# Weight conversion in a fused attention and two-layer MoE kernel: sign extraction of every third pair and more of the low parts moved from VectorE to GpSimd

## The chip, the core and the metric

The kernel runs on one core of a Trainium2 chip. TensorE multiplies matrices into PSUM; VectorE, ScalarE and GpSimd work element by element; SyncE (SP) issues the DMA transfers. The metric is the device time of one execution in microseconds, the median of several runs.

## The reference

Three steps follow each other: attention in which each query keeps its 32 best keys, a gated layer, and a layer with a squared ReLU. The attention's inputs are float32, the weights float64.

```python
def _attn_ref(q, k, v):                       # 4 batches, 8 heads, 576 x 64
    scores = scale * np.matmul(q, k.transpose(0, 1, 3, 2))
    kth = np.partition(scores, -32, axis=-1)[..., -32:-31]
    scores = np.where(scores >= kth, scores, -1000000000.0)
    scores = scores - np.max(scores, axis=-1, keepdims=True)
    attn = np.exp(scores)
    attn = attn / (np.sum(attn, axis=-1, keepdims=True) + 1e-09)
    return np.matmul(attn, v)
def _moe_ref(x, w_gate, w_val, w_out):        # x 2304 x 512, d_ff 1536
    gate = 1.0 / (1.0 + np.exp(-(x @ w_gate)))
    return (gate * (x @ w_val)) @ w_out
def _moe2_ref(x, w_in, w_out):                # d_ff 2048
    r = np.maximum(x @ w_in, 0.0)
    return (r * r) @ w_out
```

## The kernel before

The 2304 tokens are 18 row blocks of 128. Six blocks are a chunk each, the other twelve are taken in pairs (`CHUNKS`). For each chunk the attention runs over four pairs of heads, then the two layers. One head on one row block is a unit: on VectorE it is four MAX8 and three MATCH_REPLACE8 over 576 scores (L388, L395), which give the 32nd best score; GpSimd makes the small factors from it (L403, L404, L427), ScalarE the mask and the exponential (L407, L423), TensorE the scores and products.

The weights come in as float64, 128x512 to a block, two blocks to a pair; the five matrices wg, wv, wo, wi and w2 have 6, 6, 6, 8 and 8 pairs, 34 in all. `conv` makes float32 from a pair with integer arithmetic on the two 32-bit words. ScalarE copies the high word scaled by 2^-112 (L606) and the low word scaled (L625). VectorE shifts the pair left by three (L620, one operation over 128x1024) and ORs the sign of the high word into each block (L621, two operations of 128x512). GpSimd adds the low word (L626, two of 128x512). The sign is bit 31 of the high word, which is every second word of the raw tile.

Chunk 0 uses these float32 weights. For all other chunks `split` makes two float16 halves: ScalarE the high part (L661), and VectorE in one operation of 128x1024 (L664) or GpSimd in two (L666, L667) the low part. Every third low part goes to GpSimd (`LOP = 3`).

The order on each engine is not written out. A tile scheduler sets it from priorities: the code puts the weight steps, the units of the attention and the steps of chunk 0 on a time axis (`at`), and the scheduler orders each engine's queue by its own estimate. Each engine then runs its queue strictly in that order. The list of splits alternates between wg and wv, then goes to wo, wi and w2. Raw blocks and converted pairs share the slots of one pool (`WSLOTS`), so a later load waits until the add of an earlier pair has read its raw block.

For each chunk a maximum sets the scale of its input (x_1cm for chunk 1, L704) and another one that of the second layer's input (x2cm, L827); both are read on VectorE.

Of the kernel before, what the change touches and what calls it, by code (L numbers as in the profile page):

```python
# [15 lines left out]
ALU = mybir.AluOpType  # L16
# [31 lines left out]
SM2 = ()  # L48
XUP = 1000
DIAG = 2  # L50
SGN = 0
M4RAW = 0
KEYS1 = 1
SWI = 5
# [4 lines left out]
WSLOTS = 35  # L59
PREF = 4  # L60
YMOD = 0
LOP = 3
LOA = 0
TCI = 6
SB = 5
# [8 lines left out]
def tile_topk_attention__then__two_moe_layers(  # L74
# [14 lines left out]
    nc = tc.nc  # L89
# [469 lines left out]
    nblk = [0]  # L559
# [5 lines left out]
    def fetch_to(i):  # L565
        while fetched[0] < len(blocks):
            b = fetched[0]
            spare = b >= len(blocks) - M4RAW
            if b > i and not (b <= i + PREF and (spare or live[0] + 3 <= WSLOTS)):
                break  # L570
            n, kt, fb = blocks[b]
            src = weights[n][kt * P : (kt + 1) * P, fb * 512 : (fb + 1) * 512]
            pool, kw = (mpool, {"tag": "m4", "bufs": M4}) if spare else (wpool, {"tag": "w"})
            if src.dtype == F32:
                t = pool.tile([P, 512], F32, name=f"{n}_r{kt}_{fb}", **kw)
                nc.sync.dma_start(t, src)
            else:
                t = pool.tile([P, 512, 2], U32, name=f"{n}_r{kt}_{fb}", **kw)
                nc.sync.dma_start(t.rearrange("p f t -> p (f t)"), src.bitcast(U32))
            if not spare:  # L580
                live[0] += 1
            raws[(n, kt, fb)] = t
            fetched[0] += 1

    def conv(name, pi):

        pr = pairs_of[name][pi]
        fetch_to(blocks.index((name, *pr[-1])))
        if (name, pi) in CM4:
            c = mpool.tile([P, 2, 512], F32, tag="m4", bufs=M4, name=f"{name}_c{pi}")  # L590
        else:
            c = wpool.tile([P, 2, 512], F32, tag="w", name=f"{name}_c{pi}")
            live[0] += 1
        rs = [raws.pop((name, kt, fb)) for kt, fb in pr]
        ci = c.bitcast(U32)
        wide = weights[name].dtype != F32
        for e, r in enumerate(rs):
            nblk[0] += 1
            if not wide:
                nc.gpsimd.tensor_copy(c[:, e], r)  # L600
            elif YMOD and nblk[0] % YMOD == 0:
                nc.gpsimd.tensor_scalar(
                    c[:, e], r.bitcast(F32)[:, :, 1], REBIAS, 1.0, op0=ALU.mult, op1=ALU.mult
                )
            else:
                nc.scalar.activation(c[:, e], r.bitcast(F32)[:, :, 1], AF.Copy, scale=REBIAS)  # L606
        if wide:
            for e, r in enumerate(rs):
                hi = r[:, :, 1]
                if SGN and nblk[0] % SGN == 0:  # L610

                    nc.gpsimd.tensor_scalar(
                        hi.bitcast(F32), hi.bitcast(F32), 0.0, 1.0, op0=ALU.mult, op1=ALU.mult
                    )
                    nc.vector.scalar_tensor_tensor(
                        ci[:, e], ci[:, e], 3, hi, op0=ALU.logical_shift_left, op1=ALU.bitwise_or
                    )
                else:
                    if e == 0:
                        nc.vector.tensor_scalar(ci, ci, 3, None, op0=ALU.logical_shift_left)  # L620
                    nc.vector.scalar_tensor_tensor(  # L621
                        ci[:, e], hi, 0x80000000, ci[:, e], op0=ALU.bitwise_and, op1=ALU.bitwise_or
                    )
                low = r[:, :, 0].bitcast(I32)
                nc.scalar.activation(low, r[:, :, 0], AF.Copy, scale=float(2.0**-29))  # L625
                nc.gpsimd.tensor_tensor(  # L626
                    c.bitcast(I32)[:, e], c.bitcast(I32)[:, e], low, op=ALU.add
                )
        live[0] -= sum(blocks.index((name, *b)) < len(blocks) - M4RAW for b in pr)
        for e, (kt, fb) in enumerate(pr):  # L630
            flat[(name, kt, fb)] = (c, e)
# [25 lines left out]
    def split(name, pi):  # L657
# [4 lines left out]
        nsp[0] += 1  # L662
        if not (LOP and nsp[0] % LOP == 0 and nsp[0] > LOA):
            nc.vector.scalar_tensor_tensor(t[:, 1], c, s, t[:, 0], op0=ALU.mult, op1=ALU.subtract)  # L664
# [9 lines left out]
    def weight_step(n=1):  # L674
        for _ in range(min(n, len(steps) - nstep[0])):
            name, pi = steps[nstep[0]]
            conv(name, pi)
            nstep[0] += 1
            if name in ("wg", "wv", "wo") and pi == len(pairs_of[name]) - 1:
                scale(name)  # L680
# [605 lines left out]
```

## Time and profile before

| what | us |
|---|---|
| median of three runs | 1292.55 (1292.32 to 1298.61) |
| the profiled execution | 1289.27 |
| its span, first to last instruction | 1287.5 |
| TensorE matmul busy | 1175.5 (91%) |
| VectorE busy | 977.1 (76%) |
| GpSimd busy | 889.7 (69%) |
| ScalarE busy | 812.0 (63%) |

The shares are averages over stages. The stages are: up to 33 us the first keys and scores; 33 to 200 us the conversion of the weights beside the attention of chunks 0 and 1; 200 to some 310 us the splits, the end of chunk 0 and the first layer of chunk 1; from there on chunk after chunk, with the attention of a later chunk beside the layers of an earlier one, until the attention ends near 1100 us. In the rows PE is TensorE, DVE VectorE, ACT ScalarE, POOL GpSimd.

### The profile page before, as it was taken

Reading aid. Unit: us, or ns where it says so; the run is one execution under the profiler, and the core shown is the slowest. Engines: PE = TensorE matmul, PEld = TensorE weight load, DVE = VectorE, ACT = ScalarE, POOL = GpSimd, SP = SyncE. Lnnn points to the kernel's source line nnn. Section 1 sums busy time; section 2 is a strip of 40 time slices with the busy share of each in tenths; the row PEclk is TensorE's granted clock in tenths of the full one; section 3 lists DMA queues with packets and bytes.
Section 4 is the critical chain, followed back from the end, with each engine's and each line's share of the span. In section 5 each row is a group of like instructions: output and inputs, shape, how many; then the busy total and the mean of one; then the engine's idle time right before and its main releaser. Section 6 shows DMA issues by size and latency. Waiting matters only on the chain.

```text
span 1287.5 us, 31379 instructions
## 1 busy us (share of the span) xinstructions
PE 1175.5 (91%) x11709; PEld 945.3 (73%) x11709; DVE 977.1 (76%) x2002; ACT 812.0 (63%) x1714; POOL 889.7 (69%) x1454
## 2 busy tenths in 40 slices
PE   6756888877999989899998999999999999999998
PEld 5544876666887968778786778876876887787775
DVE  5999998999669987879998778999999969210010
ACT  4877777777666776667766776766676657322122
POOL 1798878876656677687876977798779759514223
PEclk9567899996999999999998999999999999999999
DMA  6978862222444346655666565556544523200000
GB/s 179 355 256 278 282 201 62 64 74 73 135 124 114 87 119 150 138 133 122 131 139 160 120 132 126 125 134 146 108 93 88 128 55 60 54 1 1 17 1 17
DMA packets 243192, 153.97 MB, mean 120 GB/s; under 512 B 193120, under 2 KB 209504, under 8 KB 243040
## 3 DMA queue, kind: packets, MB, share of 16 engines
q1 hardware_dynamic: 243040, 151.97, 45.9%
q8 instruction: 92, 1.51, 0.5%
q14 instruction: 60, 0.49, 0.1%
HBM read 105.51 MB, written 18.09 MB: 96 GB/s over the span
## 4 chain that ended last, share of the span: by engine, by line
PE 50%; DVE 20%; POOL 8%; DMA 8%; issue 6%; ACT 5%; SPq 2%; POOLq 0%; ACTq 0%; DVEq 0%
PE ph L855 11%; PE acc L876 10%; DVE mx L388 8%; DVE W L395 7%; PE pv L752 6%; PE pg L752 6%; PE acc L792 6%; PE sp L373 4%; PE xp L505 3%; DMA PT<-S 2%; PE xp L532 2%; DMA ve<-in_v_dram 1%; DMA vd<-vom 1%; POOL S L453 1%; POOL rh L868 1%
## 5 line engine op out<-in xcount | busy, mean ns | idle before, releaser
L388 DVE MAX8 mx<-W 128x8 f32<-128x576 f32 x432 | 327.3, 758 | 10.0
L395 DVE MATCH_REPLACE8 W<-mx,W 128x576 f32<-128x576 f32 x288 | 213.7, 742 | 0.0
L855 PE MATMUL ph<-x,wi_w 128*128 128x256 f16 (+1 forms) x2112 | 206.6, 251 | 5.1 <-ACT x L831 4.5
L876 PE MATMUL acc<-w_w,rh 128*128 128x512 f16 x816 | 198.5, 380 | 5.5 <-POOL rh L868 5.5
L855 PEld LDWEIGHTS <-wi_w 128*128 128x128 f16 x2112 | 170.7, 99 | 35.7 <-issue 6.2
L752 PE MATMUL pg<-xs,wg_w 128*128 128x256 f16 (+1 forms) x1584 | 158.8, 250 | 2.0 <-ACT xs L519 1.1
L752 PE MATMUL pv<-xs,wv_w 128*128 128x256 f16 (+1 forms) x1584 | 155.3, 249 | 2.6 <-DVE x2cm L827 2.5
L373 PE MATMUL sp<-kst,qt 128*128 128x288 f32 x608 | 136.2, 335 | 12.9 <-DMA kst<-ks 4.5
L407 ACT ACTIVATE W<-S,bs 128x576 f32<-128x576 f32 x144 | 111.8, 776 | 54.7 <-POOL bs L403 54.1
L752 PEld LDWEIGHTS <-wg_w 128*128 128x128 f16 x1584 | 126.9, 98 | 19.9 <-issue 1.9
L752 PEld LDWEIGHTS <-wv_w 128*128 128x128 f16 x1584 | 125.7, 98 | 18.8 <-issue 5.1
L453 POOL TENSOR_TENSOR S<-W,S 128x512 f16<-128x512 f32 x192 | 136.7, 734 | 2.1
L792 PEld LDWEIGHTS <-wo_w 128*128 128x128 f16 x1584 | 125.6, 98 | 13.1 <-issue 0.9
L876 PEld LDWEIGHTS <-rh 128*128 128x128 f16 x816 | 75.6, 98 | 78.6 <-POOL rh L868 6.8
L764 DVE TENSOR_TENSOR th<-pv,th 128x512 f32<-128x512 f32 (+1 forms) x66 | 37.0, 561 | 118.8 <-PE pv L752 117.7
L376 ACT COPY S<-sp 128x576 f32<-128x576 f32 x144 | 91.7, 637 | 55.8 <-PE sp L373 38.0
L388 DVE MAX8 mx<-S 128x8 f32<-128x576 f32 x144 | 107.0, 743 | 24.6 <-ACT S L376 24.6
L867 POOL TENSOR_TENSOR r<-r 128x512 f32<-128x512 f32 (+1 forms) x88 | 74.3, 845 | 63.4 <-ACT rh L866 57.5
L792 PE MATMUL acc<-gh,wo_w 128*128 128x128 f16 (+1 forms) x1248 | 114.3, 244 | 1.1 <-POOL gh L768 0.8
L373 PEld LDWEIGHTS sp<-kst,qt 128*128 128x128 f32 x608 | 92.4, 196 | 25.5 <-DMA kst<-ks 6.2
L395 DVE MATCH_REPLACE8 W<-mx,S 128x576 f32<-128x576 f32 x144 | 106.8, 742 | 0.0
L450 ACT ACTIVATE S<-W,rz 128x576 f16<-128x576 f32 x96 | 74.4, 775 | 48.7 <-DVE rz L446 44.9
(300 smaller groups left out, 2250.4 us busy)
## 6 DMA issues: line engine op xcount, KB each, us to landing
kst<-ks SPq DMA_DIRECT2D x112, 288.0 KB, 3.2
v<-vd SPq DMA_DIRECT2D x32, 320.0 KB, 3.2
qn<-in_q_dram SPq DMA_DIRECT2D x128, 64.0 KB, 2.6
wi_r<-in_moe_w_in_dram SPq DMA_DIRECT2D x16, 512.0 KB, 6.9
w_r<-in_moe_w_out_dram SPq DMA_DIRECT2D x16, 512.0 KB, 4.2
v<-in_v_dram SPq DMA_DIRECT2D x56, 128.0 KB, 2.4
wg_r<-in_moe_w_gate_dram SPq DMA_DIRECT2D x12, 512.0 KB, 8.0
wv_r<-in_moe_w_val_dram SPq DMA_DIRECT2D x12, 512.0 KB, 6.5
```

The source lines that it names most:

```text
L373: nc.tensor.matmul(sp[:, e, 0:HALF], l, r, start=(x == 0), stop=(x == len(ops) - 1))
L376: nc.scalar.copy(ss.rearrange("p (e s) -> p e s", e=2), sp[:, :, 0:HALF])
L388: m8 = nc.vector.max(mx[:, r], cur)
L395: nc.vector.match_replace(wk, mx[:, r], cur, NEG)
L407: nc.scalar.activation(wk, ss, AF.Prelu, bias=bs[:, 0:1], scale=1.0, alpha=BIG)
L450: nc.scalar.activation(pp[:, 0:S], wk, AF.Copy, scale=rz)
L453: nc.gpsimd.tensor_tensor(pp[:, o : o + e - f], wk[:, f:e], pp[:, f:e], op=ALU.subtract)
L752: nc.tensor.matmul(pp[:, e * N : (e + 1) * N], wblk(wd, a, c, f0, P), xs[:, b_, c, :], start=(e == 0 and n == 0), stop=(n == 3 * KM - 1), ...
L792: nc.tensor.matmul(acc[:, d // 2, (d % 2) * N : (d % 2 + 1) * N], wblk("wo", a, f, d * P, P), gh[:, b_, e * N : (e + 1) * N], start=(f == ...
L855: nc.tensor.matmul(ph[:, e * N : (e + 1) * N], wblk("wi", a, c, f0, P), x2[:, b_, c, :], start=(e == 0 and n == 0), stop=(n == 3 * KM - 1) ...
L867: nc.gpsimd.tensor_tensor(r, r, r, op=ALU.mult)
L876: nc.tensor.matmul(acc2[:, i, 0:DM], gh[:, b_, e * N + i * P : e * N + (i + 1) * P], wblk("w2", a, f, 0, DM), start=(f == 0 and x == 0), s ...
```

## The change

Of every third pair of blocks, beginning with the first, the sign is made by GpSimd: the high word, read as float32, times zero is plus or minus zero, which is the sign bit alone. VectorE then joins it with the shift in one operation (shift left by three, OR), so the pair's 128x1024 shift falls away. That is 12 of the 34 pairs. And every second low part goes to GpSimd where every third did: of 34, 17 for 11. Since wg and wv alternate in the list, these are all six of wv, none of wg.

```diff
-SGN = 0
+SGN = 3
-LOP = 3
+LOP = 2
...
         if wide:
+            signs = SGN and nblk[0] // 2 % SGN == 1
+            if not signs:
+                nc.vector.tensor_scalar(ci, ci, 3, None, op0=ALU.logical_shift_left)
             for e, r in enumerate(rs):
                 hi = r[:, :, 1]
-                if SGN and nblk[0] % SGN == 0:
+                if signs:
 
                     nc.gpsimd.tensor_scalar(
                         hi.bitcast(F32), hi.bitcast(F32), 0.0, 1.0, op0=ALU.mult, op1=ALU.mult
                     )
...
                         ci[:, e], ci[:, e], 3, hi, op0=ALU.logical_shift_left, op1=ALU.bitwise_or
                     )
                 else:
-                    if e == 0:
-                        nc.vector.tensor_scalar(ci, ci, 3, None, op0=ALU.logical_shift_left)
                     nc.vector.scalar_tensor_tensor(
```

In the changed file the shift is L610, the sign L615, the OR with the shift L618, the plain OR L622, the add L627, and GpSimd's low part L667 and L668.

VectorE's queue at the fourth and fifth pair of wv (wv_c_716 and wv_c_730 before, wv_c_719 and wv_c_734 after; mx and W belong to the attention), before:

```order
L620 TENSOR_SCALAR wv_c_716<-wv_c_716 128x1024
L395 MATCH_REPLACE W_6_782<-mx_6_783,W_6_782 128x576
L621 SCALAR_TENSOR_TENSOR wv_c_716<-wv_r_1_635,wv_c_716 128x512
L621 SCALAR_TENSOR_TENSOR wv_c_716<-wv_r_1_637,wv_c_716 128x512
L388 MAX mx_6_783<-W_6_782 128x8
L428 RECIPROCAL rz_5_707<-bs_5_702 128x1
L620 TENSOR_SCALAR wv_c_730<-wv_c_730 128x1024
L395 MATCH_REPLACE W_6_782<-mx_6_783,W_6_782 128x576
L621 SCALAR_TENSOR_TENSOR wv_c_730<-wv_r_2_649,wv_c_730 128x512
L621 SCALAR_TENSOR_TENSOR wv_c_730<-wv_r_2_651,wv_c_730 128x512
```

and after:

```order
L618 SCALAR_TENSOR_TENSOR wv_c_719<-wv_c_719,wv_r_1_638 128x512
L428 RECIPROCAL rz_5_710<-bs_5_705 128x1
L388 MAX mx_6_787<-W_6_786 128x8
L395 MATCH_REPLACE W_6_786<-mx_6_787,W_6_786 128x576
L610 TENSOR_SCALAR wv_c_734<-wv_c_734 128x1024
L388 MAX mx_6_787<-W_6_786 128x8
L388 MAX mx_7_945<-S_7_746 128x8
L622 SCALAR_TENSOR_TENSOR wv_c_734<-wv_r_2_652,wv_c_734 128x512
L622 SCALAR_TENSOR_TENSOR wv_c_734<-wv_r_2_654,wv_c_734 128x512
L618 SCALAR_TENSOR_TENSOR wv_c_719<-wv_c_719,wv_r_1_640 128x512
```

The fourth pair's shift is gone, and its second OR has moved behind the whole fifth pair.

GpSimd's queue at the same pairs (wv_r are the raw blocks, qt the queries, dg and bs the attention's factors), before:

```order
L626 TENSOR_TENSOR wv_c_653<-wv_c_653,wv_r_1_564 128x512
L349 TENSOR_TENSOR qt_0_0_756<-qn_0_663,qt_0_0_756 128x256
L427 TENSOR_SCALAR bs_5_702<-bs_5_702 128x1
L626 TENSOR_TENSOR wv_c_716<-wv_c_716,wv_r_1_635 128x512
L626 TENSOR_TENSOR wv_c_716<-wv_c_716,wv_r_1_637 128x512
L431 TENSOR_SCALAR dg_5_710<-ident,rz_5_707 128x128
L626 TENSOR_TENSOR wv_c_730<-wv_c_730,wv_r_2_649 128x512
L626 TENSOR_TENSOR wv_c_730<-wv_c_730,wv_r_2_651 128x512
```

and after:

```order
L615 TENSOR_SCALAR wv_r_1_638<-wv_r_1_638 128x512
L427 TENSOR_SCALAR bs_5_705<-bs_5_705 128x1
L627 TENSOR_TENSOR wv_c_656<-wv_c_656,wv_r_1_564 128x512
L349 TENSOR_TENSOR qt_0_0_760<-qn_0_666,qt_0_0_760 128x256
L627 TENSOR_TENSOR wv_c_656<-wv_c_656,wv_r_1_566 128x512
L615 TENSOR_SCALAR wv_r_1_640<-wv_r_1_640 128x512
L627 TENSOR_TENSOR wv_c_719<-wv_c_719,wv_r_1_638 128x512
L431 TENSOR_SCALAR dg_5_713<-ident,rz_5_710 128x128
```

The two signs of the fourth pair stand among the adds of the third, five to seven rows ahead of the adds that need them.

GpSimd's queue behind the last adds of the conversion (rr belongs to chunk 0's second layer), before:

```order
L666 TENSOR_SCALAR wg_c_305<-wg_c_305,wgs 128x1024
L431 TENSOR_SCALAR dg_7_2255<-ident,rz_7_2252 128x128
L667 TENSOR_TENSOR wg_w_1891<-wg_c_305,wg_w_1891 128x1024
L349 TENSOR_TENSOR qt_1_0_2287<-qn_1_2210,qt_1_0_2287 128x256
L666 TENSOR_SCALAR wv_c_653<-wv_c_653,wvs 128x1024
L967 TENSOR_TENSOR rr_2_2179<-r_2_2177 128x256
L667 TENSOR_TENSOR wv_w_1901<-wv_c_653,wv_w_1901 128x1024
```

and after:

```order
L667 TENSOR_SCALAR wv_c_568<-wv_c_568,wvs 128x1024
L403 TENSOR_SCALAR bs_7_2263<-mx_7_2255 128x1
L404 TENSOR_SCALAR bs_7_2263<-mx_7_2255 128x1
L668 TENSOR_TENSOR wv_w_1900<-wv_c_568,wv_w_1900 128x1024
L667 TENSOR_SCALAR wv_c_642<-wv_c_642,wvs 128x1024
L668 TENSOR_TENSOR wv_w_1907<-wv_c_642,wv_w_1907 128x1024
L349 TENSOR_TENSOR qt_1_0_2303<-qn_1_2226,qt_1_0_2303 128x256
```

The low parts on GpSimd are now wv's, and the first two follow each other directly.

## Rows read from the trace of the kernel before

**Rows 1.** Page, busy tenths in 40 slices of the span.

```profile
PE   6756888877999989899998999999999999999998
DVE  5999998999669987879998778999999969210010
```

**Rows 2.** Busy time by stage: start and end, length, each engine, TensorE's clock, DMA.

```profile
33.00:200.00 167.00, 127.78 (x945) 104.49 (x944) 161.97 (x284) 127.78 (x254) 137.26 (x133) 0.78 0.79 266
200.00:235.00 35.00, 29.16 (x197) 21.25 (x195) 31.42 (x52) 26.33 (x41) 32.48 (x29) 1.00 0.15 42
235.00:310.00 75.00, 57.55 (x652) 48.55 (x653) 72.91 (x140) 56.64 (x109) 56.41 (x88) 0.84 0.29 81
...
325.00:1100.00 775.00, 744.17 (x8234) 604.05 (x8233) 663.63 (x1433) 530.73 (x1181) 586.53 (x1098) 0.99 0.52 120
```

**Rows 3.** Timeline of VectorE, the two marks: start, duration, line, operation.

```profile
230.11 0.27 DVE L704 TENSOR_REDUCE x_1cm<-x_1pq 128x1 f32<-128x128 f32 x1
...
302.71 0.27 DVE L827 TENSOR_REDUCE x2cm<-x2pq 128x1 f32<-128x128 f32 x1
```

**Rows 4.** Shift and OR by line: ns shortest/median/longest, first and last start.

```profile
L620 DVE TENSOR_SCALAR wg_c<-wg_c x6: 677/961/1781, 33.4 to 55.2; 128x1024 uint32<-128x1024 uint32 x6
...
L621 DVE SCALAR_TENSOR_TENSOR wg_c<-wg_r,wg_c x12: 664/678/1789, 34.8 to 58.0; 128x512 uint32<-128x512 uint32 x12
```

**Rows 5.** VectorE's busy time with the shifts (L620) in the first stage.

```profile
33.00:200.00 167.00, 37.76 (x34) 0.78 0.79 266
```

**Rows 6.** VectorE's busy time with the ORs (L621) in the first stage.

```profile
33.00:200.00 167.00, 53.79 (x68) 0.78 0.79 266
```

**Rows 7.** GpSimd's busy time with the adds (L626).

```profile
33.00:201.00 168.00, 100.25 (x68) 0.78 0.79 265
```

**Rows 8.** The add (L626) of wi: ns shortest/median/longest.

```profile
L626 POOL TENSOR_TENSOR wi_c<-wi_c,wi_r x16: 1282/1408/1748, 118.3 to 155.4; 128x512 int32<-128x512 int32 x16
```

**Rows 9.** Timeline of GpSimd beside VectorE's rows 10: start, duration.

```profile
205.08 2.13 POOL L667 TENSOR_TENSOR wg_w<-wg_c,wg_w 128x1024 f16<-128x1024 f32 x1
207.17 1.71 POOL L349 TENSOR_TENSOR qt<-qn,qt 128x256 fp32r<-128x256 f32 x1
...
232.02 2.13 POOL L667 TENSOR_TENSOR wo_w<-wo_c,wo_w 128x1024 f16<-128x1024 f32 x1
...
290.08 0.73 POOL L349 TENSOR_TENSOR qt<-qn,qt 128x256 fp32r<-128x256 f32 x1
```

**Rows 10.** Timeline of VectorE at the same times: start, duration.

```profile
205.22 3.07 DVE L664 SCALAR_TENSOR_TENSOR wv_w<-wv_c,wvs,wv_w 128x1024 f16<-128x1024 f32 x1
...
231.94 0.76 DVE L388 MAX8 mx<-W 128x8 f32<-128x576 f32 x1
232.62 1.54 DVE L741 SCALAR_TENSOR_TENSOR gsc<-x_1s,wgs 128x1 f32<-128x1 f32 x1
...
289.93 0.19 DVE L741 SCALAR_TENSOR_TENSOR gsc<-x_2s,wgs 128x1 f32<-128x1 f32 x1
```

**Rows 11.** GpSimd by shape: count, busy us, mean ns, idle time before.

```profile
L437 POOL TENSOR_SCALAR W<-W,rz 128x512 f32<-128x512 f32 x32 | 22.1, 691 | 0.0
...
L667 POOL TENSOR_TENSOR w_w<-w_c,w_w 128x1024 f16<-128x1024 f32 x3 | 6.4, 2136 | 0.1
...
L716 POOL TENSOR_TENSOR xs<-xt,xs 128x512 f16<-128x512 f32 x4 | 4.6, 1160 | 0.1
...
L666 POOL TENSOR_SCALAR w_c<-w_c,w2s 128x1024 f32<-128x1024 f32 x3 | 3.4, 1117 | 1.4 <-ACT w_w L661 1.4
```

**Rows 12.** VectorE's waits for others, 200 to 315 us: total, times, longest.

```profile
DVE rz L428 <- POOL bs L427: 4.0, 3, 2.2
```

**Rows 13.** VectorE's low part (L664): ns shortest/median/longest.

```profile
L664 DVE SCALAR_TENSOR_TENSOR wi_w<-wi_c,wis,wi_w x6: 1266/1274/1519, 251.1 to 300.0; 128x1024 f16<-128x1024 f32 x6
...
L664 DVE SCALAR_TENSOR_TENSOR wv_w<-wv_c,wvs,wv_w x4: 1266/1831/3066, 202.5 to 216.8; 128x1024 f16<-128x1024 f32 x4
```

**Rows 14.** The DMA queue's (SP's) own waits, 25 to 200 us: total, times, longest.

```profile
SPq L579 <- POOL w_c L626: 12.1, 5, 3.6
```

## The prediction, before the run

> **What bounds the kernel now.** I read the busy shares in 40 slices first, then the busy time by stage, then who waits for whom. The slices show two halves: VectorE is full (nines) in the first quarter, where TensorE is not; behind it TensorE is full to the end [rows 1]. The stage table says it in numbers [rows 2]. From 33 to 200 us, where the weights are converted, VectorE is busy 162.0 of 167 us, GpSimd 137.3, TensorE 127.8. From 235 to 310 us VectorE has 72.9 of 75 us and TensorE only 57.6. From 325 to 1100 us TensorE has 744.2 of 775 us. So before 310 us the end is set by whatever keeps VectorE's queue from moving on; after 325 us the order is TensorE's, and its sequence is much the same in both kernels from the 30th score block on. A microsecond won or lost before 310 us therefore moves the end by about a microsecond, and one won on VectorE after 325 us would move nothing.
>
> Two marks cut the front. x_1cm, the maximum that scales the input of chunk 1, runs on VectorE at 230.1 us; x2cm, the one between the two layers of chunk 1, at 302.7 us [rows 3]. I call the work of one head on one row block (4 MAX8, 3 MATCH_REPLACE8) a unit, and count units in VectorE's queue.
>
> VectorE's busy time is not all work. A shift of 128x1024 takes 677 ns at its shortest, an OR of 128x512 takes 664 ns [rows 4]; the 34 shifts sum to 37.76 us [rows 5] and the 68 ORs to 53.79 us [rows 6], so 37.8 - 34 x 0.68 = 14.6 us and 53.8 - 68 x 0.66 = 8.6 us are waiting inside the instruction. GpSimd's 68 adds sum to 100.25 us [rows 7] where the shortest takes 1282 ns [rows 8]: 13 us more than 68 x 1.28 = 87.0. What they wait for stands in two places. At 205.08 GpSimd starts a low part that runs its usual 2.13 us [rows 9]; VectorE starts one at 205.22, which takes 3.07 us where 1.27 is usual and ends 1.1 us after GpSimd's [rows 10]; and the next GpSimd operation, usually 0.73 us, takes 1.71 us until VectorE is done. At 232.62 a 128x1 operation of VectorE takes 1.54 us beside another low part of GpSimd; the same line takes 0.19 us at 289.93. MAX8 beside them is not stretched. So GpSimd's operations and those of VectorE that read two SBUF tensors, or shift 1024 elements in the time of 512, take turns: there is one path for both.
>
> The Trainium skill says the same (GPSIMD Engine Reference, Key points): GpSimd shares its SBUF interfaces with VectorE and contends with its instructions in a two-port mode or with two SBUF inputs. The trace agrees: the stretched ones above are of these kinds.
>
> That path is nearly booked in the first stage: adds 87.0, shifts 23.1 and ORs 45.2 us at their shortest are 155 of 167 us, and GpSimd's other operations, recorded as 37 us, come on top. It can only fit because the edges of operations overlap. This is the point on which the case turns.
>
> **The change part by part.**
> Shifts: 12 of the 34 pairs lose theirs. VectorE saves between 12 x 0.68 = 8.2 us and, at the mean of 37.76 / 34 = 1.11 us, 13.3 us. The 68 ORs stay, and in these pairs do the shift too: same size, same two inputs, no added time.
>
> Signs: 24 new GpSimd operations, 128x512, one input, every second word. No such row exists. Below, a dense 128x512 tensor_scalar takes 691 ns [rows 11]. Above, the add that reads one operand with the same stride takes 1282 ns; a dense two-input operation of that size takes 1160 ns [rows 11], so the stride is worth some 0.12 us. I take 0.69 + 0.12 = 0.81 us, nearest to the dense row: 19.4 us, with 16.6 and 30.7 as ends.
>
> Order: in these pairs the OR now waits for GpSimd. Queued behind it on VectorE are the next MAX8 and the next pair's shift; who waits for those is GpSimd itself. The scheduler has put the two signs some rows ahead, and in one place parted the two ORs of a pair by a whole pair (wv_c_719). SP's weight loads, too, wait for GpSimd's adds to release their buffers, 12.1 us for the last matrix alone [rows 14].
>
> First stage, 33 to 200 us. VectorE falls to 149-154 us and has room. GpSimd has 137.3 + 19.4, less 12 x 0.13 us of stretch (13 us over 102 operations of VectorE), is 155.1 us. The fullest GpSimd is seen beside a busy VectorE is 32.5 of 35 us, 93%, between 200 and 235 us; there VectorE lost 4.0 us to GpSimd [rows 12]. 155.1 / 0.93 = 167 us: the stage is as long as it was. **0 us**; with the sign at 0.69 us and GpSimd without a gap 152 us, with it at 1.28 us 166.4 / 0.93 = 179 us, so -15 to +12.
>
> Low parts: 23 on VectorE and 11 on GpSimd become 17 and 17. One costs GpSimd 1.12 + 2.14 = 3.25 us [rows 11]; VectorE saves 1.27 us at the median and 1.83 where it met GpSimd [rows 13], some 1.35. wg and wv alternate in the list, so GpSimd gets all six of wv.
>
> 200 us to x_1cm: two more low parts on GpSimd (7 for 5), three fewer on VectorE (7 for 10), and x_1cm stands behind 19.25 units where it stood behind 18.25. GpSimd has 32.5 + 6.5, less 3 x 0.98 us of stretch (1.71 against 0.73 above), is 36.1 us; at 93% that is 38.8 for 35. **+4 us**; by VectorE alone, at 5.8 us a unit (72.6 us between the marks less 11 x 1.35, over 10 units), it would be 5.8 - 4.1 = +2.
>
> x_1cm to x2cm: 9.25 units for 10 and 7 low parts for 11: VectorE saves 0.75 x 5.8 + 4 x 1.35 = 9.7 us. GpSimd gets two low parts: 56.4 + 6.5 = 62.9 us [rows 2], at 93% 67.6 us of 75. The later of the two decides: **-7 us**, with 0 and -9.7 as ends. TensorE's 57.6 us fit.
>
> Sum: 0 + 4 - 7 = -3 us. The profiled execution took 1289.3 us, for which this gives 1286.3; it lies 3.3 us under the median of the three runs, 1292.55, and on that basis I forecast **1289.5 us**.
>
> **Rivals.**
> A. VectorE goes on setting the pace and GpSimd absorbs everything. For it: 162.0 of 167 us, and GpSimd's 30 us of gaps. Then the stages give -13.3 to -8.2, +2 and -9.7: -16 to -21, so 1271.5 to 1276.5, and with part of it 1284. Against it: the gaps of GpSimd are where VectorE's shifts and ORs had the path.
>
> B. The shared path decides, and the kernel is slower. An operation moved to GpSimd holds the path longer than on VectorE: 24 x 0.81 for 12 x 0.68 is +11 us, a low part 3.25 for 1.27. Place: the first stage, where GpSimd is busy 82% and the path full. It decides if GpSimd cannot get above some 88% there: 155.1 / 0.88 = 176, +9; then 36.1 / 0.88, +6; then 62.9 / 0.88 = 71.5, -3.5. Sum +11.5, so 1304, from 1299 to 1311.
>
> The Trainium skill backs this rival in GPSIMD Engine Reference, Performance versus the Vector engine: an elementwise operation takes GpSimd about twice as long as VectorE. Here the low part is 3.25 against 1.27 us, so more than that.
>
> C. That the change did not act as named can be left out: both queues show the new operations.
>
> **How the numbers follow.** My forecast, 1286 to 1299, has 0.46; A 0.29; B 0.25. A measurement of this kernel can tell about 0.5% (6.5 us) from no change, so the bounds are 1286.1 and 1299. Of A, what lies under 1277 is left out (about 0.12), of B what lies over 1304 (about 0.08): range 1277 to 1304. Faster 0.29, same 0.46, slower 0.25.
>
> **What would show it.** In the profile of the changed kernel: signs of 0.7 to 0.9 us; GpSimd over 90% busy from 33 us to the last OR, which still lies near 197 us; VectorE with waits for GpSimd's signs or reciprocals of 5 to 15 us; x_1cm near 234 us and x2cm near 300 us; behind it the same waits of TensorE. A is right if the last OR comes before 188 us and x2cm before 288; B if GpSimd's or VectorE's stretched operations fill the stage and the last OR comes after 205. I am wrong altogether if the front keeps its length and the end moves, or if the weight loads, waiting for buffers that GpSimd releases later, become what the first stage waits for.

## The result and the profile after

The changed kernel takes 1298.03 us in the median of 20 runs, the kernel before 1289.63 us in 20 runs beside it: a ratio of 1.0061 with a 95% interval of 1.0048 to 1.0073, some 8 us slower. The forecast was 1289.5 us, no measurable change. The profiled execution of the changed kernel took 1297.82 us, its span 1296.0 us.

The stage table of the changed kernel answers [rows 2] (start and end, length, then TensorE, its weight loads, VectorE, ScalarE and GpSimd with their busy time and counts, TensorE's granted clock, DMA share and rate).

```profile
33.00:200.00 167.00, 118.96 (x905) 99.82 (x904) 155.70 (x267) 123.26 (x245) 150.59 (x154) 0.80 0.79 264
200.00:235.00 35.00, 30.39 (x210) 22.41 (x210) 29.61 (x48) 25.41 (x41) 33.86 (x32) 0.99 0.17 47
235.00:310.00 75.00, 61.27 (x683) 50.60 (x683) 67.73 (x141) 56.68 (x111) 63.74 (x94) 0.87 0.27 74
325.00:1100.00 775.00, 740.92 (x8176) 601.57 (x8175) 656.52 (x1418) 528.57 (x1176) 588.01 (x1096) 0.99 0.52 119
```

GpSimd rises from 137.3 to 150.6 of 167 us in the first stage, VectorE falls from 162.0 to 155.7. The two marks of [rows 3] on VectorE's timeline:

```profile
237.27 0.29 DVE L705 TENSOR_REDUCE x_1cm<-x_1pq 128x1 f32<-128x128 f32 x1 [2.06 <-PE x_1pq L703]
...
304.56 0.27 DVE L828 TENSOR_REDUCE x2cm<-x2pq 128x1 f32<-128x128 f32 x1
```

The second mark lies 1.9 us behind that of before; the span ends 8.5 us behind. So most of the loss appears behind the place at which the prediction let the front end. Two later places show where. A unit's first MAX8 reads the raw scores (mx<-S), so these rows mark the starts of units on VectorE. I count from 0, so the first row below is unit 30 and the last unit 34. After:

```profile
316.45 0.74 DVE L388 MAX8 mx<-S 128x8 f32<-128x576 f32 x1
...
322.13 0.74 DVE L388 MAX8 mx<-S 128x8 f32<-128x576 f32 x1
322.79 1.27 DVE L665 SCALAR_TENSOR_TENSOR wi_w<-wi_c,wis,wi_w 128x1024 f16<-128x1024 f32 x1
...
327.35 0.09 DVE L395 MATCH_VALUE_LOAD W<-mx,S 128x8 f32 x1 [3.02 <-PE tp L473]
...
332.31 1.45 DVE L665 SCALAR_TENSOR_TENSOR w_w<-w_c,w2s,w_w 128x1024 f16<-128x1024 f32 x1
...
345.02 0.16 DVE L428 RECIPROCAL rz<-bs 128x1 f32<-128x1 f32 x1 [3.47 <-POOL bs L427]
346.15 0.42 DVE L765 TENSOR_TENSOR th<-pv,th 128x256 f32<-128x256 f32 x1 [0.96 <-POOL th L764]
351.36 0.16 DVE L129 TENSOR_SCALAR vs_0n<-vn 128x1 int32<-128x1 int32 x1 [4.79 <-PE vn L213]
...
358.36 0.74 DVE L388 MAX8 mx<-S 128x8 f32<-128x576 f32 x1
```

The same stretch before, with its unit 30 first and its unit 34 last:

```profile
317.96 0.74 DVE L388 MAX8 mx<-S 128x8 f32<-128x576 f32 x1
...
325.79 0.09 DVE L395 MATCH_VALUE_LOAD W<-mx,S 128x8 f32 x1 [1.41 <-PE tq L491]
...
335.77 0.16 DVE L428 RECIPROCAL rz<-bs 128x1 f32<-128x1 f32 x1 [1.80 <-POOL bs L427]
...
342.84 0.16 DVE L428 RECIPROCAL rz<-bs 128x1 f32<-128x1 f32 x1 [3.94 <-POOL bs L427]
...
346.06 0.16 DVE L129 TENSOR_SCALAR vs_0n<-vn 128x1 int32<-128x1 int32 x1 [3.06 <-PE vn L213]
...
353.89 0.74 DVE L388 MAX8 mx<-S 128x8 f32<-128x576 f32 x1
```

Four units take 41.9 us after and 35.9 before: 6.0 us are lost here. 2.7 us of that are two low parts of VectorE that stand here only after the change (1.27 and 1.45 us). Another 2.6 us are longer waits: the shown ones, with three under a microsecond that are left out, sum to 14.3 us; before, with one of 1.5 us left out, to 11.7. The low parts of this time, on both engines, are the trace's groups by line from 305 to 350 us (count, busy us, mean ns), after:

```profile
L668 POOL TENSOR_TENSOR w_w<-w_c,w_w 128x1024 f16<-128x1024 f32 x3 | 6.4, 2138 | 0.2
...
L668 POOL TENSOR_TENSOR wi_w<-wi_c,wi_w 128x1024 f16<-128x1024 f32 x1 | 2.1, 2128 | 0.0
...
L665 DVE SCALAR_TENSOR_TENSOR w_w<-w_c,w2s,w_w 128x1024 f16<-128x1024 f32 x2 | 2.7, 1362 | 0.1
L665 DVE SCALAR_TENSOR_TENSOR wi_w<-wi_c,wis,wi_w 128x1024 f16<-128x1024 f32 x1 | 1.3, 1268 | 0.0
```

and before:

```profile
L667 POOL TENSOR_TENSOR w_w<-w_c,w_w 128x1024 f16<-128x1024 f32 x1 | 2.1, 2132 | 0.1
...
L664 DVE SCALAR_TENSOR_TENSOR w_w<-w_c,w2s,w_w 128x1024 f16<-128x1024 f32 x1 | 1.3, 1259 | 0.0
```

Behind 305 us GpSimd still has four low parts for one, VectorE three for one: the splits run late.

The other place is chunk 4. The marks are the scale of its predecessor's second layer and its own (x2s_3n and x2s_4n, both on VectorE's timeline). Before:

```profile
453.56 0.15 DVE L129 TENSOR_SCALAR x2s_3n<-x2cm 128x1 int32<-128x1 int32 x1
...
528.89 0.13 DVE L129 TENSOR_SCALAR x2s_4n<-x2cm 128x1 int32<-128x1 int32 x1
```

and after:

```profile
455.18 0.13 DVE L129 TENSOR_SCALAR x2s_3n<-x2cm 128x1 int32<-128x1 int32 x1
...
538.29 0.14 DVE L129 TENSOR_SCALAR x2s_4n<-x2cm 128x1 int32<-128x1 int32 x1
```

Before needs 75.3 us from one to the other, the changed kernel 83.1 us. Nothing of the change's work is left there. The loss of the attention had not simply been handed on to this place: unit 34 starts 4.5 us late, but the scale of chunk 2's second layer (x2s_2n) comes only 0.5 us late, at 383.4 us, and x2s_3n 1.6 us. One wait in chunk 4, on TensorE's timeline (start, duration, idle time before and its releaser):

```profile
485.25 1.50 PE L753 MATMUL pv<-xs,wv_w 128*128 128x128 f16 x24
489.82 2.25 PE L877 MATMUL acc<-w_w,rh 128*128 128x512 f16 x6 [3.07 <-POOL rh L869]
491.87 2.30 PE L753 MATMUL pg<-xs,wg_w 128*128 128x128 f16 x22
```

and what GpSimd did meanwhile:

```profile
486.35 2.79 POOL L453 TENSOR_TENSOR S<-W,S 128x512 f16<-128x512 f32 x4
489.10 0.67 POOL L869 TENSOR_TENSOR rh<-r,rh 128x256 f16<-128x256 f32 x1
```

Four operations of the attention (L453) stand in GpSimd's queue ahead of the one that TensorE waits for. Such a group stands ahead of one in the kernel before too (475.65 to 478.45 us, with a wait of TensorE of 1.64 us behind it), so this wait differs in length and not in kind. This is an example; what shows that the step goes with the order are e4 to e6 below. The order has changed far beyond the weights: behind x2cm of chunk 1, 836 of TensorE's 9,697 matmuls have another successor than before, 395 of some 1,150 operations on VectorE and 592 of 1,191 on GpSimd (counted in the two programs' queues).

### The profile page after: what moved, and what is told of

Read it like the earlier page. It is cut to its first block, busy times and chain, and to the rows that moved or that the text cites. A ratio compares the mean times of both kernels' runs of the same rounds, so it can differ in the third digit from the quotient of the medians.

```text
span 1296.0 us, 31420 instructions
## 1 busy us (share of the span) xinstructions
PE 1173.5 (91%) x11709; PEld 942.9 (73%) x11709; DVE 965.9 (75%) x1984; ACT 811.4 (63%) x1714; POOL 924.1 (71%) x1490
## 4 chain that ended last, share of the span: by engine, by line
PE 38%; POOL 12%; DVE 9%; DMA 6%; issue 4%; ACT 3%; SPq 1%; POOLq 0%; ACTq 0%; DVEq 0%
PE ph L856 7%; PE acc L877 7%; PE pv L753 6%; PE acc L793 6%; PE pg L753 6%; DVE mx L388 4%; DVE W L395 4%; PE sp L373 3%; POOL S L453 2%; PE xp L505 2%; DMA PT<-S 2%; POOL rh L869 2%; POOL r L868 2%; DMA vd<-vom 1%; POOL W L451 1%
## 5 line engine op out<-in xcount | busy, mean ns | idle before, releaser
L877 PE MATMUL acc<-w_w,rh 128*128 128x512 f16 x816 | 200.6, 382 | 7.6 <-POOL rh L869 7.5
L753 PE MATMUL pv<-xs,wv_w 128*128 128x256 f16 (+1 forms) x1584 | 158.1, 249 | 2.7 <-ACT th L763 2.2
L453 POOL TENSOR_TENSOR S<-W,S 128x512 f16<-128x512 f32 x192 | 136.7, 733 | 2.4
L877 PEld LDWEIGHTS <-rh 128*128 128x128 f16 x816 | 76.5, 98 | 81.7 <-POOL rh L869 9.1
```

The source lines that it names most:

```text
L453: nc.gpsimd.tensor_tensor(pp[:, o : o + e - f], wk[:, f:e], pp[:, f:e], op=ALU.subtract)
L753: nc.tensor.matmul(pp[:, e * N : (e + 1) * N], wblk(wd, a, c, f0, P), xs[:, b_, c, :], start=(e == 0 and n == 0), stop=(n == 3 * KM - 1), ...
L877: nc.tensor.matmul(acc2[:, i, 0:DM], gh[:, b_, e * N + i * P : e * N + (i + 1) * P], wblk("w2", a, f, 0, DM), start=(f == 0 and x == 0), s ...
```

## The experiments

Two theories stood against each other first. *Work*: the loss is the price of what was moved. *Order*: the front is about neutral, and the loss comes from the queues that the scheduler drew up anew behind it. Later the work theory became narrower (*tail*): the price is that of the low parts behind 305 us.

All ratios are to the kernel before, timed beside each kernel. "16", "30", "34" are the starts of those units on VectorE against before (199.6, 318.0, 353.9 us), from one profiled execution each; "30 to 34" is the difference, what is lost between the two. The control n50 has before's queues, but for a few rows, and lies 1 us ahead of it at all three, so a microsecond is scatter. The execution that was profiled need not be a typical one: n20's took 1290.14 us, the shortest of its seven (median 1297.55), and e7's 1295.54 us, the longest of its ten (median 1290.78). So the ends are compared by the ratios.

| kernel | signs | low parts | ratio (95%) | 16 | 30 | 34 | 30 to 34 |
|---|---|---|---|---|---|---|---|
| changed | yes | every 2nd | 1.0061 (1.0048 to 1.0073) | +4.3 | -1.5 | +4.5 | 6.0 |
| e1 | yes | every 3rd | 1.0099 (1.0077 to 1.0120) | +5.0 | +2.7 | +2.5 | -0.2 |
| e2 | no | every 2nd | 1.0078 (1.0061 to 1.0095) | -0.4 | -4.7 | +3.1 | 7.8 |
| e3, change's work | yes | every 2nd | 1.0171 (1.0152 to 1.0189) | +4.9 | +21.3 | +21.4 | 0.1 |
| e4, before's work | no | every 3rd | 1.0030 (1.0010 to 1.0051) | -1.3 | -3.2 | +0.2 | 3.4 |
| e5, change's work | yes | every 2nd | 1.0038 (1.0016 to 1.0061) | +4.4 | -1.2 | +4.9 | 6.0 |
| e6, before's work | no | every 3rd | 1.0028 (1.0010 to 1.0047) | -0.2 | -0.2 | +0.2 | 0.4 |
| e7, before's work | no | every 3rd | 0.9999 (0.9981 to 1.0017) | -0.2 | -2.1 | +1.3 | 3.4 |
| e8 | no | every 2nd | 1.0042 (1.0017 to 1.0066) | -1.3 | -5.7 | +4.5 | 10.2 |
| n34 | no | every 3rd | 1.0078 (1.0056 to 1.0100) | -3.6 | -2.8 | -1.9 | 0.8 |
| n4 | no | every 3rd | 1.0019 (1.0000 to 1.0038) | -4.1 | -3.2 | -1.5 | 1.7 |
| n20 | no | every 3rd | 1.0056 (1.0038 to 1.0074) | +1.6 | -1.5 | -2.5 | -1.0 |
| n50, control | no | every 3rd | 1.0003 (0.9985 to 1.0022) | -1.3 | -1.0 | -0.9 | 0.0 |
| c4 | yes | every 2nd | 1.0084 (1.0069 to 1.0100) | +2.0 | -2.0 | +5.0 | 7.0 |
| c20 | yes | every 2nd | 1.0069 (1.0051 to 1.0086) | +4.5 | +1.1 | +7.4 | 6.3 |
| c34 | yes | every 2nd | 1.0068 (1.0053 to 1.0083) | +6.7 | -0.6 | +6.2 | 6.8 |
| c50 | yes | every 2nd | 1.0093 (1.0076 to 1.0109) | +4.8 | +2.7 | +8.7 | 6.0 |
| f1 | no | 2nd, then 3rd | 1.0012 (0.9992 to 1.0031) | -1.5 | -6.3 | -5.0 | 1.3 |
| f2 | no | 3rd, then 2nd | 1.0013 (0.9995 to 1.0031) | -1.0 | -2.8 | +1.9 | 4.7 |

**e1 and e2: one half of the change each.**

```diff
 # e1, against the changed kernel
-LOP = 2
+LOP = 3
 # e2, against the changed kernel
-SGN = 3
+SGN = 0
```

> The signs on GpSimd as in the change (12 of 34 pairs), but every third low part as before. Work theory (the loss is the price of the moved work): the signs are the new GpSimd load of the first stage, so the last OR comes 3 us later than before, and most of the loss is here, ratio near 1.005. Order theory (the front is neutral, and the loss comes from the queues that the scheduler drew up behind 310 us): x2cm of chunk 1 within 3 us of before (302.7), and the end anywhere within 10 us of before, on either side, with a jump of several us between two later chunks that has no tie to the front.

> Every second low part on GpSimd as in the change, no signs. Work theory: the first stage as before, x_1cm some 4 us later, x2cm up to 7 us earlier, and the end 3 us before to 4 us after that of before. Order theory: the same front, but the end is drawn anew, within 10 us of before on either side, and does not follow x2cm.

Each half alone is slower than both together, 1.0099 and 1.0078: effects of the two that were added up would give 1.018, not 1.006. By the work theory that makes no sense; by the order theory it may. Yet e1 lies outside the order theory's bounds as well: its x2cm is 3.8 us late, where 3 were allowed, and its end 13 us, where 10 were. And in e2, x_1cm did not move (230.0 us), where both theories had the front's 4 us. But the units hold something of the work theory. The signs cost 5 us by unit 16, as the changed kernel does, and keep 2.5 of it. The low parts alone bring 4.7 us by unit 30, a gain as the prediction counted it on VectorE, and lose 7.8 in the next four units.

**e3 to e8: the queues held.** In front of a chosen place the scheduler is free; behind it each engine's queue is held to a listed order by edges that set the order of issue only.

```diff
+def pin_order(tc, nc):
+    here = {i.name: i for i in nc.cur_bb.bb.instructions}
+    for steps in json.loads(zlib.decompress(base64.b85decode(ORDER))).values():
+        n, prev = 0, None
+        for step in steps:
+            n += step
+            cur = here[f"I-{n}"]
+            if prev is not None:
+                tc.add_manual_dep(cur, prev.name, NOSYNC, reason="listed order")
+            prev = cur
...
         tile_topk_attention__then__two_moe_layers(tc, *args)
+        pin_order(tc, nc)
```

> The change whole, but behind x2cm of chunk 1 each engine's queue is held to the order that it has in the kernel before; in front of it all is as in the change. Order theory: x2cm near 304.6 us, the step of 8 us between chunks 3 and 4 is gone, and the end lies 2 us behind before (ratio 1.0015, at most 1.003). Work theory: the loss stays, ratio 1.006.

> The kernel before, with none of the change's operations, but behind x2cm of chunk 1 each engine's queue is held to the order of the changed kernel. Order theory: x2cm near 302.7 us, the step of 8 us between chunks 3 and 4 appears here too, ratio 1.005 to 1.006. Work theory: as before, ratio 1.000.

e3 took 1.0171 (1.0152 to 1.0189) and told nothing of either theory: the place was badly chosen. The list begins amid the last low parts, whose order differs in the two kernels, and TensorE stood at that seam (its waits, 305 to 330 us):

```profile
PE sp L373 <- ACT S L376: 19.6, 1, 19.6
```

Unit 30 starts 21.3 us late there and the span ends 23.2 us late, so behind the seam the old order lost no more than 2 us. e4 has before's work and the new order: 1.0030, half of what order theory expected. The step in chunk 4 is there (450.0 to 533.6, 83.6 us), but the stretch from x2s_1n to x2s_2n became 4.5 us shorter.

> As e3, but the queues are held to the order of the kernel before only behind x2cm of chunk 2 (near 383 us), where both kernels stand within 0.4 us of each other and the last low parts are done; in e3 the held order began in the middle of them, and TensorE lost 19.6 us there at one place. Order theory: the change whole, with the old order behind 383 us, ends 0 to 3 us behind before, ratio 1.000 to 1.002. Work theory (what the change costs in the front comes out late, whatever the order): the end stays 8 us behind, ratio 1.006.

> The mirror of e5: the kernel before, with the order of the changed kernel behind x2cm of chunk 2. Order theory: level with before at 383 us, 6 to 9 us behind it from x2cm of chunk 4 on, ratio 1.005 to 1.007. Work theory: ratio 1.000.

Here the seam is clean. Neither theory's number came: 1.0038 for the change's work under the old order, 1.0028 for before's work under the new one. That is some 4.9 us and 3.6 us, and the sum, 8.5 us, is close to the changed kernel's 7.9 (0.61% of 1290), though each of the two is known to some 3 us only. Both theories are half right. Chunk 4's step goes with the order: in e6, before's work under the new order,

```profile
451.50:534.70 83.20, 70.58 (x970) 59.39 (x967) 66.55 (x159) 56.55 (x140) 60.56 (x121) 1.00 0.56 126
```

and in e5, the change's work under the old order (columns as in the stage table; each window runs from x2s_3n to x2s_4n):

```profile
458.40:536.90 78.50, 69.55 (x944) 59.76 (x944) 58.34 (x143) 53.63 (x128) 57.11 (x111) 0.96 0.52 125
```

83.2 and 78.5 us; n50, with before's work and order, takes 78.3, so 3 us of scatter lie between it and the 75.3 us of before. In all nine kernels that have either of the two orders here the step follows the order and not the work: 75.3 to 79.3 us with the old one (before, n50, e3, e5, e7, e8), 83.1 to 83.6 with the new one (the changed kernel, e4, e6).

> The kernel before, with the order of the changed kernel only between x2cm of chunk 1 and x2cm of chunk 2 (303 to 383 us), its own order in front and behind. In e4 this stretch took 73.7 us where before it takes 78.2. Order theory: the gain of 4 us stays to the end, ratio 0.996 to 0.998, faster than both kernels. If a gain in one stretch is lost at the next seam: ratio 1.000 or above.

> The low parts alone (no signs), with the order of the kernel before behind x2cm of chunk 2. Alone they were 1.9 us ahead of before at that place and 9.7 us behind at the end. Order theory: the 1.9 us stay, ratio 0.998 to 1.000. Work theory: 1.007, as with its own order.

e7 is level with before: at the second scale of chunk 2 (x2s_2n) it stood 2.2 us ahead, and that was gone by chunk 3 (x2s_3n 2.0 us behind). It is also a control for e5: its queues are held from 303 us on, with the same change to the old order at 383 us, and its work is before's. So e5's 0.38% is not the price of holding the queues. But e5 has the order that the scheduler drew for the change up to 383 us, and no run has the change's work there in the old order: the 0.38% belong to the work and its order in front together. e8, at 1.0042, has the old order from 383 us on and is slower all the same, against the order theory's expectation: at unit 34, in front of the held order, it is already 4.5 us late (though at x2s_2n, 382.6 us, it is level with before again).

**n34, n4, n20, n50: an operation that does nothing.** The kernel before, with one more VectorE operation, at the 17th, second, tenth or 25th pair; for the second it reads

```diff
+    pad = const.tile([P, 1], F32, name="pad")
...
+        if nblk[0] == 4:
+            nc.vector.tensor_scalar(pad, c[:, 1, 0:1], 1.0, None, op0=ALU.mult)
```

> The kernel before plus one VectorE operation of 128x1 (some 0.2 us) that reads the 17th converted pair; its result is used nowhere. No work moves. The scheduler's queues differ from before's on all engines from this place to the end. Order theory: the front moves by less than 4 us, and the end anywhere within 10 us, most likely later, since the order of before is one that turned out well: ratio 1.002 to 1.008. Work theory: 0.2 us, ratio 1.000.

> As n34, the one operation at the second pair instead; another set of queues, different from before's over two thirds of the program. Order theory: ratio 1.002 to 1.008, with steps at other chunks than in n34. Work theory: 1.000.

> As n34, the one operation at the tenth pair; the queues differ from before's up to some two thirds of the program and are the same behind. Order theory: ratio 1.002 to 1.008. Work theory: 1.000.

> The control for the three others: the same operation at the 25th pair, where the queues stay those of before but for a few rows around it. Both theories: ratio 1.000, within 0.002.

In n34 the operation is this one (ns shortest/median/longest, then its start in us):

```profile
L631 DVE TENSOR_SCALAR pad<-wo_c x1: 136/136/136, 111.7 to 111.7; 128x1 f32<-128x1 f32 x1
```

0.14 us of work that nobody reads make the kernel 0.78% slower, some 10 us, because the scheduler's estimate shifts and it draws other queues on all engines. n20 loses 0.56%, n4 0.19%, and the control, in which the same operation leaves the queues almost as they were, 0.03%. The order theory's expectation held for n34 and n20, and n4 lies at its edge. Where the loss comes also follows the draw: at unit 34 n34 is 1.9 us ahead of before, and its span ends 11.1 us late.

**c4, c20, c34, c50: the changed kernel under other orders**, with the same two lines.

> The changed kernel plus one VectorE operation of 128x1 at the second pair, which draws the queues anew. If the change's own work costs nothing and its 0.6% are those of the order it got, the changed kernel under new orders spreads as the kernel before under new orders does (ratios 1.002 to 1.008 in n34, n4, n20), with a mean near theirs, 1.005. If the work costs some 0.6% on top, the mean is near 1.010 and none lies under 1.006.

> As c4, the operation at the tenth pair: work neutral, 1.002 to 1.008; work dear, 1.006 to 1.014.

> As c4, the operation at the 17th pair: work neutral, 1.002 to 1.008; work dear, 1.006 to 1.014.

> As c4, the operation at the 25th pair: work neutral, 1.002 to 1.008; work dear, 1.006 to 1.014.

With the changed kernel these are five orders of the same work: 1.0061 to 1.0093, mean 1.0075. Before's work under the three new orders has a mean of 1.0051. The difference, 0.24%, is within what three and five draws scatter, so the ends leave it open whether the work itself costs anything. The units say more, up to unit 34: in all five, and in e5, it starts 4.5 to 8.7 us behind before, and in the seven kernels with before's work (e4, e6, e7 and the four n) from 2.5 us ahead to 1.3 behind. Between units 30 and 34 eight of the nine kernels with every second low part lose 6.0 to 10.2 us. The ninth, e3, loses 0.1, but it comes there out of a stop of 20 us, in which GpSimd could catch up. Those with every third lose at most 1.7, and 3.4 in e4 and e7, which have the changed kernel's order there. So up to unit 34 the kernel is later with the change's work under every order that was drawn, and more than half of the 6.0 us also comes with the order alone. That these microseconds reach the end is not shown.

**f1 and f2: early or late low parts.**

```diff
 # f1, against the kernel before
-        if not (LOP and nsp[0] % LOP == 0 and nsp[0] > LOA):
+        if nsp[0] % (2 if nsp[0] <= 24 else 3):
 # f2, against the kernel before
+        if nsp[0] % (3 if nsp[0] <= 24 else 2):
```

> The kernel before, with every second low part on GpSimd only among the first 24 of the 34 and every third behind (15 in all); no signs. Tail theory: the low parts that GpSimd still has to do behind 305 us (four in the changed kernel, one before) hold back the attention between its units 30 and 34, by 6 to 10 us in every run with every second low part, by 2 at most in the others. Here the 30th unit comes 4 to 6 us earlier than before, as with low parts alone, and 2 to 4 us of that are kept at the 34th; the end is then 0.4% behind to 0.3% ahead, as the new order falls. If the tail is not the cause, unit 34 is 3 us or more behind before, as with low parts alone.

> The mirror: every third low part on GpSimd among the first 24 of the 34, every second among the last ten (13 in all); no signs. Its queues are those of before up to some 260 us. Tail theory: level with before at the 24th unit, and 4 to 8 us lost between the 30th and the 34th, although only two low parts more than before are on GpSimd; ratio 1.003 to 1.008. If the tail is not the cause: unit 34 within 2 us of before.

f1 has 15 low parts on GpSimd, four more than before. It keeps 5.0 of the 6.3 us that it is ahead at unit 30. f2 has two more than before and loses 4.7 us in these four units; that it then stands at +1.9 us, just inside the bound given for "not the cause", is because it came in 2.8 us ahead, and its ratio, 1.0013, is below the 1.003 expected. So in this pair, too, the stretch is lost where every second of the last ten low parts is GpSimd's, and not where it is the early ones. That the low parts in the stretch are themselves the cost is not shown, and their number speaks against it: behind 305 us f1 and n4 each have three on VectorE and two on GpSimd, and lose 1.3 and 1.7 us; f2 has one and two, and loses 4.7. By which wait the time is lost is not settled either. GpSimd is busy 17.5 of 18 us between 318 and 336 us in the changed kernel and 9.6 before, but in f1, which loses little, it is 17.1.

And f1's 5.0 us do not reach the end either: at x2s_3n it is 7.1 us ahead of before, at x2s_5n 6.6 us behind. No kernel that was tried beats the kernel before: the nearest, e7, n50, f1 and f2, can't be told from it.

## Why the prediction was wrong

**The step that failed** is the premise under the sum: "A microsecond won or lost before 310 us therefore moves the end by about a microsecond", with the front cut at x2cm, and TensorE's sequence behind it taken as "much the same". The prediction named this case itself: "I am wrong altogether if the front keeps its length and the end moves". It did: +1.9 us at x2cm, +8.5 at the end. Nor does the end follow x2cm in the other runs: e2 has x2cm 2.5 us earlier than before and its end 9.7 us later, n34 1.6 us earlier and 11.1 us later. The front's own sum failed as well, by 5 us (-3 forecast); the terms are below. Two things were left out of the sum.

The first is the work behind the second mark, with what comes with it. The prediction counted the low parts up to x2cm and never asked where the rest of the 17 and 17 lie. By their starts in the two traces, VectorE has 14 up to x2cm where it had 21, and three behind it for two; GpSimd has 13 for 10, and four behind it for one. So one of the seven that VectorE seemed to lose was only put off, and three of GpSimd's six new ones lie behind the mark. Behind x2cm the attention then loses 6.0 us in four units; by which wait, and how much of it reaches the end, stays open. e5 puts the price of the work, together with the order that it got up to 383 us, at 0.38%, 4.9 us.

The second is the order behind the front: 0.28%, 3.6 us, in e6, and 0.2 to 0.8% for a draw that moves no work at all. This part the runs show on its own, with no work moved. I had judged it by the counts of score blocks at which TensorE starts each tile, which hide the order inside, and had not looked at the queues of the engines that feed TensorE. The evidence was to be had: the queues of both kernels can be compared without a run. The price of such a draw cannot be read from them, but it belongs in the sum as a term of its own: with the 0.2 to 0.8% of n4, n20 and n34 on top, which were measured only afterwards, the forecast of 1289.5 would have been 1292 to 1300.

The terms one by one, by the front's own marks:

- *First stage, 0 us.* The last OR starts 2.9 us later (the last number of the ORs' rows of the last matrix, after and before), unit 16 starts 4.3 us later. This is the signs: the last OR starts 3.6 us late in e1, which has them alone, and 0.3 us early in e2, which has none. GpSimd was as full as forecast, just over 90% (150.6 of 167 us), though the sum had 155.1 us for it.

```profile
L618 DVE SCALAR_TENSOR_TENSOR w_c<-w_c,w_r x6: 878/1132/1410, 164.8 to 200.6; 128x512 uint32<-128x512 uint32 x6
```

```profile
L621 DVE SCALAR_TENSOR_TENSOR w_c<-w_r,w_c x16: 664/683/1678, 158.0 to 197.7; 128x512 uint32<-128x512 uint32 x16
```

- *The sign, 0.81 us.* It takes 0.65 us where it is undisturbed, under the lower end of 0.69 (shortest/median/longest ns of the signs of two matrices):

```profile
L615 POOL TENSOR_SCALAR wi_r<-wi_r x6: 645/652/717, 117.0 to 150.4; 128x512 f32<-128x512 f32 x6
...
L615 POOL TENSOR_SCALAR wv_r<-wv_r x4: 647/1082/1097, 57.4 to 77.9; 128x512 f32<-128x512 f32 x4
```

- *The shifts, and "the 68 ORs stay ... no added time".* Half right. Busy time up to 230 us in the changed kernel, by line: the shifts left (L610), the signs (L615), the ORs with the shift (L618), the plain ORs (L622):

```profile
0.00:230.00 230.00, 22.94 (x22) 0.85 0.69 224
...
0.00:230.00 230.00, 17.70 (x24) 0.85 0.69 224
...
0.00:230.00 230.00, 26.32 (x24) 0.85 0.69 224
...
0.00:230.00 230.00, 40.30 (x44) 0.85 0.69 224
```

  VectorE saves 37.8 - 22.9 = 14.8 us of shifts, more than the 13.3 allowed. But its ORs grow from 53.8 [rows 6] to 26.3 + 40.3 = 66.6 us, though the shortest of both kinds still take 0.67 us. So 12.8 of the 14.8 us are given back, as waiting inside the instruction. The signs do it: the same two lines sum to 66.6 us in e1, with the signs alone, and the 68 ORs to 53.8 us in e2, without them. That is the shared path of the prediction, at work where it put no price: GpSimd's signs are new traffic on it. In one place, GpSimd's sign and VectorE's OR:

```profile
57.42 1.07 POOL L615 TENSOR_SCALAR wv_r<-wv_r 128x512 f32<-128x512 f32 x1
```

```profile
57.91 1.12 DVE L622 SCALAR_TENSOR_TENSOR wg_c<-wg_r,wg_c 128x512 uint32<-128x512 uint32 x1
```

  The OR begins 0.5 us behind the sign and ends 0.5 us after it. The Trainium skill has the rule (SBUF — State Buffer, Summary: rules for kernel authors): if VectorE has two inputs in SBUF while a GpSimd operation reads SBUF, the later of the two is blocked until the first is done. The trace agrees in these two rows, and the sign has a single input. By that rule the change could relieve VectorE's count but not the path. The 12.8 us are the term that the prediction should have put on the ORs.
- *200 us to x_1cm, +4 us.* From 200.6 to 237.3 us, where before went from 197.7 to 230.1: +4.3. The number came out, but not for the reason given. The prediction put it on the low parts; with the low parts alone (e2) the stretch is 0.2 us longer than before, and under the four other orders of the same work (c4, c20, c34, c50) it takes 31.1 to 35.2 us, 1.3 us less to 2.8 more. That it fits is luck.
- *x_1cm to x2cm, -7 us.* 67.3 us for 72.6: -5.3, inside its ends. This, too, is one draw: e2 takes 70.2 us, the four c kernels 70.8 to 74.3. None of the kernels with the change's work reached the forecast's 300 us at x2cm; they have it at 303.7 to 310.1.
- *Waits of VectorE for signs and reciprocals, 5 to 15 us.* 1.7 us for signs and 4.9 for reciprocals, 6.6 in all (VectorE's waits, 33 to 202 us: total, times, longest):

```profile
DVE rz L428 <- POOL bs L427: 4.9, 3, 3.4
...
DVE w_c L618 <- POOL w_r L615: 1.1, 2, 0.6
...
DVE wi_c L618 <- POOL wi_r L615: 0.6, 1, 0.6
```

**The rivals.** A fell: the last OR did not come before 188 us. B named the right sign and nearly the time (1299 to 1311, measured 1298), but not the place: its condition, GpSimd held under 88% in the first stage, was not met, and its -3.5 us between the marks was -5.3. Only the part on the shared path lives on, in the ORs. Neither rival had what happens behind x2cm or the order.

## What to carry to other kernels

Where a scheduler sets the queues, compare them to the end of the program, not around the edit alone, and time an operation that does nothing beside the change: only what exceeds that draw is the change's. By this measure the ends do not tell this change from a draw: it lost 0.61%, the operation that does nothing 0.19 to 0.78%. Follow moved work until it is all done: a mark ahead of its last operation shows a gain that may only be postponed. And an operation that leaves an engine frees nothing if its replacement uses the path on which that engine waits.

## What the runs showed of the hardware

GpSimd's one-input operation on every second word (128x512, 0.65 us) is no slower than the dense one of that size, 0.69 us [rows 11], and half as long as its add with one strided operand (1.28 us [rows 8]).

The wait of 3.07 us at 486.8 us in the changed kernel cost TensorE more than its length. In the windows 486 to 490 and 490 to 494 us the granted clock, the third column from the end, is

```profile
486.00:490.00 4.00, 0.93 (x15) 0.69 (x13) 2.13 (x5) 0.83 (x3) 3.92 (x7) 1.00 0.24 45
490.00:494.00 4.00, 4.00 (x28) 2.78 (x27) 3.65 (x8) 1.77 (x4) 3.26 (x6) 0.57 0.77 154
```

1.00 and 0.57: having worked 0.93 us of the first window, TensorE ran for most of the second at the lower of its two levels, 1.2 GHz (an estimate from the mean of 0.57). Six matmuls of L877 took 2.25 us where six take 1.47 us at 479.6 us before (L876), behind a wait of 1.64 us:

```profile
479.63 1.47 PE L876 MATMUL acc<-w_w,rh 128*128 128x512 f16 x6 [1.64 <-POOL rh L868]
```

There the granted clock stayed at 1.00:

```profile
480.00:484.00 4.00, 4.00 (x44) 2.75 (x42) 2.75 (x6) 3.07 (x6) 3.47 (x7) 1.00 0.66 135
```

So of two waits for the same producer the longer cost its own length and slower matmuls behind it.
